# Paced first loads, and halves of the partitions exchanged by copies, in a gated mix of linear attention and a squared-ReLU MLP

## The chip, the cores and the metric

One core of a Trainium2 chip runs the whole program. The metric is device time of one execution, in microseconds (us); the times shown are the median of three runs. A profile is a further execution, with its own time. In its rows PE is TensorE's products and PEld its weight loads, DVE is VectorE, ACT ScalarE, POOL GpSimd, SP the engine that issues most transfers.

## The reference

x has 2048 rows of 448 columns. Two branches read it, and a gate for each row mixes them:

```python
qkv = (x @ wqkv).reshape(B, S, 3, 16, 28)            # q, k, v by head
phi = lambda t: where(t > 0, t + 1, exp(t)) + 1e-6
kv = einsum("bhsd,bhse->bhde", phi(k), v);  z = einsum("bhsd->bhd", phi(k))
a = (phi(q) kv / (phi(q) z + 1e-6)) @ wo             # heads joined
b = relu(x @ w1 + b1) ** 2 @ w2 + b2                 # 448 -> 1792 -> 448
g = sigmoid((x * gate_w).sum(-1))
out = g * a + (1 - g) * b
```

All in float32.

## The kernel before

**Arithmetic.** Each float32 operand is split into a rounded high part and the rest, and a product is taken as high x high, high x low and low x high. Splitting is two instructions: a cast (ScalarE or VectorE) for the high part and a subtraction (VectorE) for the low one. The 448 columns stand as four blocks of 128, the last 64 columns twice, so that the last block's high and low part use the two halves of the rows of the array.

**TensorE.** It is used as two halves of 64 rows. Each product of 128 rows is issued as two of 64, one for each half, and the halves have their own order of work (`stream[0]`, `stream[1]`). `LO` and `UP` are partitions 0 to 63 and 64 to 127.

**Stages.** Phase one takes the four blocks of 512 rows in turn: the first seven of 14 blocks of hidden units (`h_ps`, banks tagged `mm`), their down products (`o_ps`, tag `acc`), keys (`k_ps`) and the products of keys with x (`g_ps`). Then come key sums (`z_ps`), the small kv matrix, its product with wo (`kv_ps`, `m_ps`); then the blocks again for the other hidden units, queries (`q_ps`), denominators (`d_ps`) and attention (`a_ps`). Keys, queries, denominators and attention share two banks of PSUM with tag `ms`.

**What sets the order.** Nothing is ordered at run time. `Flow` is a planner: it holds a queue of operations for each engine and two lists of products, simulates them with a table of costs, and emits every instruction in the order in which the simulation starts it. `FIRST` tells it when the first 256, 512, 768 and 1024 KB have landed; `stream` starts at the time when the first product may begin; `SHIFT`, `MOVE` and `LEAVE` are tables of numbers that move single operations. Every engine then runs its list in order and waits on semaphores. The recording of all operations is one line (285) and that of all products another (420).

**The start.** TensorE begins with 15 products of 256 columns on a constant, into a bank nobody reads (line 683). SP issues eight loads of 256 KB one after the other: two that hold the first columns of w1 and x (`in_first`), then w1 and x for the other three blocks of columns, in turn. ScalarE casts the high parts; VectorE subtracts. Before the first real products the planner fills a wait with further products nobody reads (`filler`, line 684), as long as its clock is below `FILLED`.

**Halves exchanged.** At three places a sum over both halves of the partitions is needed in both: the key sums (`key_sums`), the last block of the queries (`queries_done`, `c == 3`) and the denominators' sums. There each half is transferred into the other half of another buffer by SP, and VectorE adds the two. SP's list is in order too: a transfer that waits for its data holds the loads behind it.

Of the kernel before, what the change touches and what calls it, by code (L numbers as in the profile page):

```python
# [11 lines left out]
ALU = mybir.AluOpType  # L12
# [14 lines left out]
def f32(ap):  # L27
# [8 lines left out]
FAST, FIRST = 5.2, ((262144, 3.42), (524288, 4.05), (786432, 5.1), (1048576, 6.1))  # L36
OVERLAP = {"act": 0.1, "dve": 0.085, "pool": 0.05, "sp": 0.0}

FILLED = 5.5
# [4 lines left out]
SHIFT = {"a_ps0": 7, "a_ps10": 3, "a_ps11": -10.5, "a_ps12": 11.5, "a_ps15": 10, "a_ps3": 3, "a_ps6": -1.5, "a_ps7": 26,  # L44
# [20 lines left out]
MOVE = {"a_ps0": 0.5, "a_ps1": 1.5, "a_ps10": 1.5, "a_ps12": 1.5, "a_ps13": 1.5, "a_ps14": 1, "a_ps15": -0.5, "a_ps3": 0.5,  # L65
# [11 lines left out]

LEAVE = {"a_ps0": 0, "a_ps13": -0.3, "a_ps14": 1, "a_ps15": 0.6, "a_ps2": 0.6, "a_ps3": 0.6, "a_ps5": 1, "a_ps7": 0.6,
# [13 lines left out]


class Bank:
# [89 lines left out]
class Flow:  # L184
# [138 lines left out]
    def candidate(self, name):  # L323
        best = None
        for k, op in enumerate(self.queues[name][:60]):
            if any(x.end is None for x in op.after):
                continue
# [204 lines left out]
def gated_mix_kernel(ctx: ExitStack, tc: tile.TileContext, first_in, xt, xn, wk, wq, wv, wo, w1a, w1b, w2, b1, b2, gw, hmask,  # L532
# [161 lines left out]
    for c in range(1, 4):  # L694
        load_w1(0, 0, c)
        load_x(0, c)
# [684 lines left out]
```

## Time and profile before

| what | value |
|---|---|
| median of three runs | 431.21 us (431.02 to 431.22) |
| the profiled execution | 430.65 us |
| its span, first to last instruction | 428.7 us |
| TensorE products, share of the span | 99% |
| VectorE, ScalarE | 62%, 46% |
| transfers, mean | 71 GB/s |

The span leaves out what lies before the first and after the last instruction: 1.95 us here. A row of a timeline gives start, length, engine, line, operation and shapes; in square brackets stands how long the engine was idle before and what ended it. Rows that follow each other are merged (x30), and a length then reaches from the first one's start to the last one's end. A group of instructions gives the busy time and the mean of one in ns, then the idle time before them by what ended it. A transfer's time runs from issue to landing.

### The profile page before, as it was taken

Reading aid. Unit: us, or ns where it says so; the run is one execution under the profiler, and the core shown is the slowest. Engines: PE = TensorE matmul, PEld = TensorE weight load, DVE = VectorE, ACT = ScalarE, POOL = GpSimd, SP = SyncE. Lnnn points to the kernel's source line nnn. Section 1 sums busy time; section 2 is a strip of 40 time slices with the busy share of each in tenths; the row PEclk is TensorE's granted clock in tenths of the full one; section 3 lists DMA queues with packets and bytes.
Section 4 is the critical chain, followed back from the end, with each engine's and each line's share of the span. In section 5 each row is a group of like instructions: output and inputs, shape, how many; then the busy total and the mean of one; then the engine's idle time right before and its main releaser. Section 6 shows DMA issues by size and latency. Waiting matters only on the chain.

```text
span 428.7 us, 9431 instructions
## 1 busy us (share of the span) xinstructions
PE 424.9 (99%) x3966; PEld 411.5 (96%) x3966; DVE 267.9 (62%) x517; ACT 197.2 (46%) x345; POOL 16.7 (4%) x38
## 2 busy tenths in 40 slices
PE   9999999999999999999999999999999999999997
PEld 7999999999999999999999999999999999999996
DVE  5998154934677326783764739979727695259524
ACT  6974245532365324562554456643444453364331
POOL 0000000000000000000006710000000000000000
PEclk9999999999999999999999999999999999999999
DMA  8825210141111302422325550121210310012002
GB/s 287 283 96 139 67 50 2 47 122 45 49 32 47 86 28 59 113 69 78 102 63 121 100 151 2 25 69 44 75 50 2 112 26 0 2 26 88 2 0 87
DMA packets 19802, 30.52 MB, mean 71 GB/s; under 512 B 2816, under 2 KB 14128, under 8 KB 19760
## 3 DMA queue, kind: packets, MB, share of 16 engines
q1 hardware_dynamic: 18352, 28.32, 21.5%
q0 software_dynamic: 1408, 1.61, 2.2%
q8 instruction: 31, 0.51, 0.5%
q14 instruction: 11, 0.09, 0.1%
HBM read 22.31 MB, written 3.67 MB: 61 GB/s over the span
## 4 chain that ended last, share of the span: by engine, by line
PE 99%; DVE 0%; issue 0%
PE h_ps L420 34%; PE o_ps L420 30%; PE q_ps L420 9%; PE g_ps L420 8%; PE k_ps L420 8%; PE a_ps L420 7%; PE kv_ps L420 1%; PE warm_ps L683 1%; PE m_ps L420 1%; PE e_ps L420 0%; PE d_ps L420 0%; PE z_ps L420 0%; DVE slot L285 0%; PE warm_ps L684 0%
## 5 line engine op out<-in xcount | busy, mean ns | idle before, releaser
L420 PE MATMUL h_ps<-x,w 64*128 64x512 f32 (+1 forms) x1178 | 253.8, 394 | 0.0
L420 PE MATMUL o_ps<-w_all,slot 64*128 64x448 f32 x1323 | 223.2, 361 | 0.0
L420 PEld LDWEIGHTS h_ps<-x,w 64*128 64x128 f32 x1178 | 195.0, 185 | 5.3 <-ACT w L285 0.6
L420 PEld LDWEIGHTS o_ps<-w_all,slot 64*128 64x128 f32 x1323 | 196.2, 184 | 3.3 <-PE o_ps L420 0.3
L285 DVE TENSOR_TENSOR slot<-slot,slot 128x512 fp32r<-128x512 f32 (+5 forms) x122 | 80.9, 676 | 35.4 <-ACT slot L285 24.5
L285 ACT ACTIVATE slot<-h_ps,few 128x512 f32<-128x512 f32 x56 | 38.3, 687 | 92.5 <-PE h_ps L420 82.8
L285 ACT ACTIVATE slot<-slot 128x512 f32<-128x512 f32 (+2 forms) x108 | 67.0, 628 | 9.5 <-DVE slot L285 4.7
L420 PE MATMUL q_ps<-x,wq_s 64*128 64x512 f32 x308 | 67.4, 393 | 0.0
L420 PE MATMUL k_ps<-wkm,x 64*128 64x448 f32 x336 | 66.9, 360 | 0.0
L420 PEld LDWEIGHTS k_ps<-wkm,x 64*128 64x128 f32 x336 | 57.8, 184 | 0.6
L420 PE MATMUL g_ps<-p,nh 64*128 64x448 f32 x256 | 58.3, 359 | 0.0
L420 PE MATMUL a_ps<-wkm,q 64*128 64x448 f32 x336 | 57.2, 360 | 0.0
L420 PEld LDWEIGHTS q_ps<-x,wq_s 64*128 64x128 f32 x308 | 51.4, 184 | 1.6 <-PE q_ps L420 0.3
L420 PEld LDWEIGHTS a_ps<-wkm,q 64*128 64x128 f32 x336 | 51.2, 184 | 0.6
L420 PEld LDWEIGHTS g_ps<-p,nh 64*128 64x128 f32 x256 | 42.0, 184 | 0.5
L285 DVE TENSOR_SCALAR slot<-slot 128x512 f32<-128x512 f32 (+1 forms) x35 | 14.2, 408 | 36.7 <-ACT slot L285 36.4
L420 PE MATMUL g_ps<-p,nl 64*128 64x448 f32 x96 | 31.1, 360 | 0.0
L285 ACT ACTIVATE slot<-k_ps 128x448 f32<-128x448 f32 x30 | 15.1, 541 | 31.2 <-PE k_ps L420 30.5
L285 ACT ACTIVATE slot<-q_ps 128x512 f32<-128x512 f32 x26 | 15.0, 596 | 25.7 <-PE q_ps L420 24.4
L285 POOL DMA_DIRECT2D wkm<-m x32 | 16.3, 518 | 231.0 <-ACT m L285 227.0
L285 DVE TENSOR_TENSOR gsum<-g_ps,gsum 128x448 f32<-128x448 f32 x12 | 7.5, 624 | 24.2 <-PE g_ps L420 24.2
L285 DVE CAST slot<-slot 128x512 fp32r<-128x512 f32 (+2 forms) x21 | 8.4, 401 | 21.2 <-ACT slot L285 20.9
(77 smaller groups left out, 308.2 us busy)
## 6 DMA issues: line engine op xcount, KB each, us to landing
slot<-in_xt SPq DMA_DIRECT2D x27, 256.0 KB, 2.8
slot<-in_xn SPq DMA_DIRECT2D x16, 224.0 KB, 2.6
out<-slot SPq DMA_DIRECT2D x15, 224.0 KB, 1.9
slot<-in_w SPq DMA_DIRECT2D x14, 224.0 KB, 2.8
slot<-slot SPq DMA_DIRECT2D x16, 128.0 KB, 2.4
slot<-in_w1a SPq DMA_DIRECT2D x7, 256.0 KB, 3.4
slot<-in_w1b SPq DMA_DIRECT2D x8, 192.0 KB, 3.8
wkm<-m POOLq DMA_DIRECT2D x24, 56.0 KB, 2.3
```

The lines of the kernel that those rows point to most:

```text
L285: return (lambda: method(*[real(x) for x in args], **{k: real(x) for k, x in kwargs.items()}), *self.cost(name, kind, out, ins, args))
L420: ins = pe.matmul(b.ps[where or b.whole], real(a), real(m), start=b.seen == 1 + j.whole, stop=b.seen == b.total)
L683: pe.matmul(warm_ps[:, :256], warm[:, :P], warm, start=True, stop=True)
```

## The change

Five things are done.

1. The 15 wide warm-up products become 26 of 128 columns, and `filler` goes.
2. The second to fifth load of SP wait for one of these products each (the 4th, 10th, 16th and 21st), so that SP issues them some 0.6 us apart; what stands behind on SP follows. `FIRST` and the start of `stream` get earlier times.
3. The three exchanges of halves are made by two copies of 64 partitions each, by ScalarE or VectorE as the planner chooses. For the queries the copies read PSUM, and the copy of the whole bank into SBUF goes.
4. The loads of `kvmask` and `hmask` are cut in two.
5. The planner's three tables are new, so that the order of many operations on all engines differs.

```diff
-FAST, FIRST = 5.2, ((262144, 3.42), (524288, 4.05), (786432, 5.1), (1048576, 6.1))
+FAST, FIRST = 5.2, ((262144, 2.95), (524288, 3.6), (786432, 4.3), (1048576, 5.0))
...
-FILLED = 5.5
+START = 3.45
...
-SHIFT = {"a_ps0": 7, "a_ps10": 3, "a_ps11": -10.5, "a_ps12": 11.5, "a_ps15": 10, "a_ps3": 3, "a_ps6": -1.5, "a_ps7": 26,
+SHIFT = {"a_ps0": 7, "a_ps1": 6, "a_ps11": -13.5, "a_ps12": 11.5, "a_ps15": 10, "a_ps3": 3, "a_ps4": -1.5, "a_ps6": -1.5,
...
     def candidate(self, name):
...
-            if any(x.end is None for x in op.after):
+            if any(x.end is None for x in op.after) or self.queues[name][0].behind and not op.behind:
                 continue
-            ready = max([self.now] + [x.end + SIGNAL for x in op.after])
+            ready = max([self.now] + [x.end + SIGNAL for x in op.after] + [op.behind[0] if op.behind else 0.0])
...
-        self.tc.keep_in_program_order(emit())
+        ins = self.tc.keep_in_program_order(emit())
+        if op.behind and op.behind[1]:
+            self.tc.add_manual_dep(ins.ins, op.behind[1], AFTER, reason="the loads before it keep the transfers busy")
...
     def start(self, s, j, start):
-        if start < FILLED and None is self.current[0] is self.current[1]:
-            for _ in range(int((start - max(self.stream)) / 0.107)):
-                self.tc.keep_in_program_order(self.filler())
...
-        self.stream, self.current, self.left = [3.95, 3.95], [None, None], {}
+        self.stream, self.current, self.left = [START, START], [None, None], {}
...
-    for _ in range(15):
-        pe.matmul(warm_ps[:, :256], warm[:, :P], warm, start=True, stop=True)
-    flow.filler = lambda: pe.matmul(warm_ps[:, :P], warm[:, :P], warm[:, :P], start=True, stop=True)
+    warm_up = []
+    for _ in range(26):
+        ins = pe.matmul(warm_ps[:, :P], warm[:, :P], warm[:, :P], start=True, stop=True)
+        warm_up.append(ins.ins.name)
...
+    for n, op in enumerate(flow.queues["sp"]):
+        at = 0.7 + 0.6 * min(n, 4)
+        op.behind = at, warm_up[round((at - 0.83) / 0.1067) - 1] if 0 < n < 5 else None
...
     def key_sums():
         for p in (0, 64):
-            load(r[p:p + 64], ksum[(p ^ 64):(p ^ 64) + 64])
+            copy(r[p:p + 64], ksum[(p ^ 64):(p ^ 64) + 64])
...
-            load(kvm[0], kvmask)
+            for n in (0, D // 2):
+                load(kvm[0][:, n:n + D // 2], kvmask[:, n:n + D // 2])
...
     def queries_done(b, c, ps):
         if c == 3:
-            v = slot(TB)
-            copy(v, ps)
             for p in (0, 64):
-                load(r[p:p + 64], v[p ^ 64:(p ^ 64) + 64])
-            dve.tensor_tensor(v, v, r, op=ALU.add)
+                copy(r[p:p + 64], ps[p ^ 64:(p ^ 64) + 64])
+            dve.tensor_tensor(r, ps, r, op=ALU.add)
             close(r)
-            ps, r = v, slot(TB)
-            close(v)
+            ps, r = r, slot(TB)
...
             for p in (0, 64):
-                load(r[p:p + 64], total[(p ^ 64):(p ^ 64) + 64])
+                copy(r[p:p + 64], total[(p ^ 64):(p ^ 64) + 64])
```

What the planner makes of it, at three places. In these rows `w10` is the split w1, `x0` and `x1` the high and low part of x, and a name in brackets is what the row waits for (`PE_49` TensorE, `DMAHW` a transfer, `Activation_49` ScalarE).

The first loads on SP, before and now:

```order
L285 DMA slot0_147<-in_first 128x512
L285 DMA slot1_155<-in_first 128x512
L285 DMA slot2_158<-in_w1a 128x512
L285 DMA slot3_160<-in_xt 128x512
L285 DMA slot4_162<-in_w1a 128x512
L285 DMA slot5_164<-in_xt 128x512
```

```order
L288 DMA slot0_158<-in_first 128x512
L288 DMA slot1_167<-in_first 128x512 [waits PE_49]
L288 DMA slot2_169<-in_w1a 128x512 [waits PE_49]
L288 DMA slot3_171<-in_xt 128x512 [waits PE_49]
L288 DMA slot4_175<-in_w1a 128x512 [waits PE_49]
L288 DMA slot5_180<-in_xt 128x512
```

The order of the loads is the same; four of them now wait for TensorE. The order of the casts and subtractions on ScalarE and VectorE, up to the split of `wkm`, is the same too.

The first real products on TensorE, before and now (each row is one half of the rows):

```order
L420 MATMUL h_ps0_0_173<-x0_75,w10_79 128x256 [waits DVE_49,Activation_49]
L420 MATMUL h_ps0_1_175<-x0_75,w10_79 128x256
L684 LDWEIGHTS const-bfloat16-1.0
L684 MATMUL warm_ps_85<-const-bfloat16-1.0 128x128
L684 LDWEIGHTS const-bfloat16-1.0
L684 MATMUL warm_ps_85<-const-bfloat16-1.0 128x128
L420 MATMUL h_ps0_0_173<-x0_75,w10_79 128x256 [waits Activation_49]
L420 MATMUL h_ps0_1_175<-x0_75,w10_79 128x256
L420 MATMUL h_ps0_3_189<-x0_75,w10_79 128x512 [waits Activation_49]
```

```order
L425 MATMUL h_ps0_0_178<-x0_75,w10_79 128x256 [waits DVE_49,Activation_49]
L425 MATMUL h_ps0_0_178<-x0_75,w10_79 128x256 [waits Activation_49]
L425 MATMUL h_ps0_3_193<-x0_75,w10_79 128x512 [waits Activation_49]
L425 MATMUL h_ps0_2_195<-x0_75,w10_79 128x512
L425 MATMUL h_ps0_0_178<-x1_76,w10_79 128x512 [waits DVE_49]
```

The bank `h_ps0_1`, which filled the upper half of the rows, and the fillers have left this place. Ahead of the first full-wide product, which waits for ScalarE's third cast, only the two products of `h_ps0_0` in the lower half remain. Fourteen full-wide products stand from there to the first one that reads the third and fourth load.

The fold of the first queries' last block on VectorE, now (its bank `q_ps3_3`; ahead of these rows ScalarE has made the other copy):

```order
L288 COPY slot7_3249<-q_ps3_3_3176 64x512 [waits Activation_49]
L288 TENSOR_TENSOR slot7_3249<-q_ps3_3_3176,slot7_3249 128x512 [waits DVE_49]
L288 TENSOR_TENSOR x0_75<-slot11_3222,x1_76 128x512 [waits DMAHW1_49,Activation_49]
L288 TENSOR_SCALAR slot0_3269<-slot0_3269 128x512 [waits Activation_49]
L288 TENSOR_TENSOR slot0_3269<-slot0_3269,slot1_3276 128x512 [waits DVE_49,Activation_49]
```

VectorE's copy waits for ScalarE's, and the sum for both, so the bank is read three times in a row where it was read once.

More of the change, by code (lines that the diff above doesn't have):

```diff
@@ L34 @@
 LATE, SIGNAL, TO_PE, LANDING, MOVED, SPREAD, HANDED, WAITED = 0.19, 0.04, 0.12, 1.7, 1.4, 4.0, 0.24, 0.1
-FAST, FIRST = 5.2, ((262144, 3.42), (524288, 4.05), (786432, 5.1), (1048576, 6.1))
+FAST, FIRST = 5.2, ((262144, 2.95), (524288, 3.6), (786432, 4.3), (1048576, 5.0))
 OVERLAP = {"act": 0.1, "dve": 0.085, "pool": 0.05, "sp": 0.0}
-FILLED = 5.5
+START = 3.45
 AFTER = mybir.DependencyInfo(mybir.DependencyClass.Sync, mybir.DependencyReason.DATA)
-SHIFT = {"a_ps0": 7, "a_ps10": 3, "a_ps11": -10.5, "a_ps12": 11.5, "a_ps15": 10, "a_ps3": 3, "a_ps6": -1.5, "a_ps7": 26,
[20 rows of a table removed]
-MOVE = {"a_ps0": 0.5, "a_ps1": 1.5, "a_ps10": 1.5, "a_ps12": 1.5, "a_ps13": 1.5, "a_ps14": 1, "a_ps15": -0.5, "a_ps3": 0.5,
[11 rows of a table removed]
-LEAVE = {"a_ps0": 0, "a_ps13": -0.3, "a_ps14": 1, "a_ps15": 0.6, "a_ps2": 0.6, "a_ps3": 0.6, "a_ps5": 1, "a_ps7": 0.6,
[13 rows of a table removed]
+SHIFT = {"a_ps0": 7, "a_ps1": 6, "a_ps11": -13.5, "a_ps12": 11.5, "a_ps15": 10, "a_ps3": 3, "a_ps4": -1.5, "a_ps6": -1.5,
[22 rows of a table added]
+MOVE = {"a_ps0": 0.5, "a_ps10": 1, "a_ps12": 1.5, "a_ps13": 1.5, "a_ps14": 1.5, "a_ps15": -0.5, "a_ps2": 1, "a_ps3": 0.5,
[11 rows of a table added]
+LEAVE = {"a_ps0": 0.15, "a_ps13": -0.3, "a_ps14": 1, "a_ps15": 0.6, "a_ps2": 0.6, "a_ps3": 0.6, "a_ps5": 1, "a_ps7": 0.6,
[14 rows of a table added]
 class Bank:
@@ L127, in __init__ @@
         self.takes, self.size, self.end = takes, size, None
-        self.leave, self.late = 0.0, 0.0
+        self.leave, self.late, self.behind = 0.0, 0.0, None
 class Hold:
@@ L1233, in before1 @@
                 raw = slot(P)
-                load(raw, hmask)
+                for n in (0, P // 2):
+                    load(raw[:, n:n + P // 2], hmask[:, n:n + P // 2])
                 split_hi(act, hm, raw)
```

91 rows, old and new, of tables (LEAVE, MOVE, SHIFT) are left out of this document.

## The prediction

> **What bounds the kernel now.** I read the page first: its head, the busy shares, and the chain that ended last.
>
> ```profile
> span 428.7 us, 9431 instructions
> PE 424.9 (99%) x3966; PEld 411.5 (96%) x3966; DVE 267.9 (62%) x517; ACT 197.2 (46%) x345; POOL 16.7 (4%) x38
> PE 99%; DVE 0%; issue 0%
> ```
>
> TensorE sets the end from the first microsecond to the last. So only two things can change the time: when its real products begin, and how often they wait. "Busy" does not tell the second, since a waiting product can hide behind one still draining; I count products against time instead. The chain of waits in order of time gives the steady pace; the groups of the first 10 us, shapes apart, give the count there; and the stretches up to 7.42 us (columns: length, PE, PEld and ACT busy, clock, DMA share, GB/s) split it.
>
> ```profile
> 404.55 2.33 PE h_ps L420 x20
> L420 PE MATMUL h_ps<-x,w 64*128 64x512 f32 x36 | 5.0, 409 | 0.0
> L420 PE MATMUL h_ps<-x,w 64*128 64x256 f32 x4 | 1.2, 577 | 0.0
> 4.00:5.28 1.28, 0.95 (x4) 0.66 (x6) 0.00 (x0) 1.00 1.00 306
> 5.28:7.42 2.14, 2.14 (x20) 1.93 (x19) 0.00 (x0) 1.00 1.00 348
> ```
>
> Steady: 2.33 / 20 = 0.1165 us a product (two run side by side, one in each half of the rows). By 10 us, 36 full and 4 half-wide products are worth 36 x 0.1165 + 4 x 0.058 = 4.43 us. The first began at 4.07 (next fence), so 5.93 us passed and **1.50 us** were lost. Up to 5.28 only the 4 half-wide ones ran: 0.23 us of work in 1.21, so 0.98 of the loss; the other 0.52 came later. After 10 us the list of waits has, for TensorE, little:
>
> ```profile
> PEld o_ps L420 <- PE o_ps L420: 0.3, 1, 0.3
> PEld h_ps L420 <- PE h_ps L420: 0.3, 1, 0.3
> PEld q_ps L420 <- PE q_ps L420: 0.3, 1, 0.3
> ```
>
> The h_ps one belongs to the start and the o_ps one to the last tiles, where the rows stop being split; the q_ps one, which the same view still has for 262 to 276 us alone, is the only stall of the middle. So all that this change can win is about 1.5 + 0.3 us, and part of the 1.5 is a price of the slow start, which stays. Now the start itself, in order of time:
>
> ```profile
> 0.74 0.85 SPq L285 DMA_DIRECT2D slot<-in_first  x2
> 0.78 3.36 PE L683 MATMUL warm_ps<-const-bfloat16-1.0 128*128 128x256 bf16 x15 [0.78 <-PEq L1373]
> 1.65 0.42 SPq L285 DMA_DIRECT2D slot<-in_w1a  x1
> 2.11 0.43 SPq L285 DMA_DIRECT2D slot<-in_xt  x1
> 3.50 0.42 ACT L285 ACTIVATE w<-slot 128x256 fp32r<-128x256 f32 x1 [1.48 <-DMA slot<-in_first]
> 4.07 0.58 PE L420 MATMUL h_ps<-x,w 64*128 64x256 f32 x2
> 4.10 0.42 ACT L285 ACTIVATE x<-slot 128x256 fp32r<-128x256 f32 x1 [0.19 <-DMA slot<-in_first]
> 4.43 0.40 ACT L285 ACTIVATE w<-slot 128x256 fp32r<-128x256 f32 x1
> 4.58 0.40 PE L684 MATMUL warm_ps<-const-bfloat16-1.0 128*128 128x128 bf16 x2
> 4.91 4.45 PE L420 MATMUL h_ps<-x,w 64*128 64x256 f32 x30
> 5.95 0.63 ACT L285 ACTIVATE w<-slot 128x512 fp32r<-128x512 f32 x1 [1.13 <-DMA slot<-in_w1a]
> 6.62 0.69 DVE L285 TENSOR_TENSOR w<-slot,w 128x512 fp32r<-128x512 f32 x1 [1.30 <-ACT w L285]
> ```
>
> Load, ScalarE's cast, product: the first load lets ScalarE begin at 3.50, the second at 4.10, the third only at 5.95, 4.3 us after its issue at 1.65. The warm-up products step (3.36 - 0.42) / 14 = 0.21 us for 256 columns, where a steady product takes 0.233 in its half for 512: half pace. At 5.28:7.42 the pace is full (20 rows, two of them left over from before: 18 in 2.14, 0.119 each). So half pace ends near 5.3.
>
> **The change part by part.** First, **pacing**. A load that met little else, and the third and fourth as issued now:
>
> ```profile
> DMA to landing us min/median/max: 2.6/2.8/5.3
> slot<-in_first SPq DMA_DIRECT2D x2, 256.0 KB, 2.8
> slot<-in_w1a SPq DMA_DIRECT2D x1, 256.0 KB, 4.3
> slot<-in_xt SPq DMA_DIRECT2D x1, 256.0 KB, 4.5
> 3.00:3.50 0.50, 1.00 1.07 401
> 3.50:4.00 0.50, 1.00 0.95 279
> 4.50:5.00 0.50, 1.00 0.83 283
> 8.50:9.00 0.50, 1.00 1.08 399
> ```
>
> (The first row is of all 27 loads of x, 256 KB each; the last four are stretches with clock, DMA share and GB/s.) The first load took 2.74, near the best seen: even alone it lands at 0.74 + 2.6 = 3.34 at the earliest, against 3.48. The planner's new table says 2.95; no load of this size in the trace was that quick, so I take 3.35. The second now waits for the 4th warm-up product. These are 128 wide, so they step 0.107; the two fillers of that width run 0.30 (0.40 for two, less the step). The 4th ends at 0.78 + 3 x 0.107 + 0.30 = 1.40, so the issue moves from 1.17 (0.74 + 0.43) to about 1.45. With 2.6 to 2.9 it lands at 4.05 to 4.35; now 4.08. I take 4.1: no gain. The third waits for the 10th (0.78 + 9 x 0.107 + 0.30 = 2.04, issue 2.1), the fourth for the 16th (2.69, issue 2.75), the fifth for the 21st (3.22, issue 3.27, now 2.59); the rest follow at 0.47 each on SP, so everything queued behind them is issued 0.7 later. If 2.6 to 2.9 holds for them too, the third lands at 4.7 to 5.0 (now 5.93) and the fourth at 5.35 to 5.65 (now 6.57). The bandwidth would allow it: the rate falls from 401 to 280 GB/s just when all eight are queued, and comes back later.
>
> [...]
>
> **The start.** The first product can begin at 3.37 + 0.42 + 0.15 (the lag of 3.92 to 4.07 now) = 3.9. But the order shows that ahead of ScalarE's third cast only one bank's products stand there, in one half of the rows; both halves run in full once that cast is done: second load 4.1 + 0.42 + 0.40 + 0.08 = 5.0 (now 4.91, by the same sum). Work done by 5.28: at half pace (5.28 - 5.0) / 2 = 0.14, and 0.23 / 2 for the one half's two products, 0.26 in all, against 0.23 now. So nothing up to there. After it, the waits for the third to sixth load: ScalarE's cast of the third ends near 5.5 instead of 6.58, the fourth's near 6.2 instead of 7.22, VectorE's first subtraction at 5.5 instead of 6.62. The first product on them is due after 14 others of full width: 5.28 + 14 x 0.1165 - 0.14 = 6.8. The 0.52 us should go; I keep 0.1 for VectorE, whose second subtraction ends near 6.9. **-0.42**, between +0.6 (landings late by the whole delay of issue) and -0.7 (the planner's landings, below).
>
> Would VectorE give it back later? From 10 to 20 us it is the tightest engine:
>
> ```profile
> 10.00:20.00 10.00, 10.00 (x95) 9.74 (x92) 9.79 (x20) 9.37 (x19) 0.00 (x0) 1.00 0.93 316
> ```
>
> 9.79 of 10 busy. But its chain began at 6.62 after 1.30 idle, and that start moves up by 1.0, more than the 0.42 that TensorE asks.
>
> **Copies for transfers.** Out go 16 transfers of 128 KB and 2 a little smaller, all in the second half, and four copies out of PSUM; in come 18 copies of 64 partitions, and two loads are cut in two. Prices, by the group of the nearest shape and the view of the q_ps tile:
>
> ```profile
> slot<-slot SPq DMA_DIRECT2D x16, 128.0 KB, 2.4
> L285 DVE CAST slot<-slot 128x512 fp32r<-128x512 f32 x18 | 7.7, 425 | 21.1 <-ACT slot L285 20.9
> L285 ACT ACTIVATE slot<-q_ps x26: 579/597/602, 218.9 to 375.6; 128x512 f32<-128x512 f32 x26
> L285 DVE TENSOR_SCALAR slot<-q_ps x2: 692/692/692, 230.0 to 303.4; 128x512 f32<-128x512 f32 x2
> 260.00:310.00 50.00, 50.00 (x463) 47.51 (x461) 43.76 (x74) 24.87 (x43) 0.00 (x0) 1.00 0.15 46
> ```
>
> No row has 64 partitions crossing; I take the 128-partition price (0.42 to 0.69 each, some 18 x 0.6 - 4 x 0.6 = 8.4 us over two engines and half the span), since the length of a row, not the number of rows, is what the same groups differ by; twice that would be 20 us. It hides: TensorE holds the end, and even in the fullest 50 us VectorE idles 6.2 and ScalarE 25. A query's fold shortens from 0.6 + 2.4 + 0.69 = 3.7 to 0.60 + 0.69 + 0.69 = 2.0, off the path. But its PSUM bank, free after 0.60 now, is held those 2.0 us: +1.4, four times. **0.0**, between 0 and +1.4 for each bank that TensorE needs sooner.
>
> **The new list.** It can lose the 0.3 stall or bring others; I take **-0.05**, between -0.3 and +0.6. Sum: -0.42 + 0 - 0.05 = -0.47. Span 428.7 to 428.2; with the 1.95 us around it, the profiled 430.65 becomes 430.2. The median is 431.21, 0.56 above that execution, so I forecast **430.7**.
>
> **The rivals.** 0.2% of 431.2 is 0.86 us, about what a measurement of this kernel can tell from no change.
>
> A, the planner's landings are right: 2.95 and 3.6. Then both halves run from 3.6 + 0.9 = 4.5, and by 5.28 have 0.39 + 0.12 = 0.51 against my 0.26: 0.25 more, and if the 0.3 stall also goes, about -1.0: **430.2**. For it: the drop to 280 GB/s. Against: 2.6 is the least flight seen. 0.24.
>
> B, pacing only delays: the third load flies 4.3 however late it starts, because the engines and not the queue are slow. Then all splits come 0.4 to 0.7 later: +0.5, **431.7**, within 0.2%. Against it: 2.6 to 2.8 for loads of the same size later on. 0.13.
>
> C, the slower side, the clock. The rule that fills waits before the first products with warm-up products is gone; 26 steps of 0.107 end at 3.56, and until 5.0 TensorE issues two narrow products (0.21 each) in half its rows: 1.0 us empty. If full pace has to be earned anew, from 5.0 for as long as now (0.78 to 5.3, 4.5 us), half pace lasts to 9.5: (9.5 - 5.3) / 2 = +2.1, **432.8**. It decides if that 1.0 us counts as idle. Against: now, of the 1.21 us from 4.07 to 5.28, two pairs and two fillers fill only 2 x 0.21 + 2 x 0.107 = 0.63, and 0.58 is empty. 0.07. [...]
>
> D, also slower: the bank held 1.4 us longer meets a product that needs it. One such wait is -0.47 + 1.4 = +0.9, **432.1**. For it: TensorE takes its products in a written order. Against: the planner knows the bank as taken until the last reader. 0.10.
>
> **How the numbers follow.** Forecast 0.46, with its own range 430.3 to 431.1, of which 0.04 lies beyond 0.86 us; A 0.24, B 0.13, C 0.07, D 0.10. Faster by over 0.2%: 0.28. Within: 0.42 + 0.13 = 0.55. Slower: 0.17. From 429.8 (A with 0.4 to spare) to 432.2 only C and the ends of A and D are left out.
>
> **What would show it.** Right: first cast at 3.4, second near 4.1, third near 4.9; some 4 more products begun by 10 us (0.42 / 0.1165); VectorE's first wide subtraction near 5.5. Wrong: a second cast before 3.8 (A), a third after 5.8 (B), products of 0.23 us steps after 6 us (C), TensorE waiting on VectorE or ScalarE at a q_ps bank after 214 us (D).

## The result, and the profile after

The changed kernel takes **433.47 us** (median of four, 433.07 to 433.71) against 431.12 (430.77 to 431.22) for the kernel before beside it: ratio 1.0057, 95% interval 1.0045 to 1.0070. It is slower by 2.35 us, where 430.7 was forecast. The profiled execution took 433.71 us, its span 431.9 where before's was 428.7. It is the slowest of the four, and before's profile (430.65) is quicker than before's median, so what the two traces differ by, 3.27 us, is more than 2.35.

The page's head and busy shares:

```profile
span 431.9 us, 9393 instructions
PE 427.6 (99%) x3975; PEld 413.1 (96%) x3975; DVE 274.8 (64%) x532; ACT 198.0 (46%) x344; POOL 16.7 (4%) x38
```

TensorE is as "busy" as before, and the span is 3.2 us longer: a share of 99% cannot show the loss. The start in order of time (SP's issues, TensorE's warm-up, then ScalarE's casts):

```profile
0.74 0.98 SPq L288 DMA_DIRECT2D slot<-in_first  x2
0.78 2.93 PE L686 MATMUL warm_ps<-const-bfloat16-1.0 128*128 128x128 bf16 x26 [0.78 <-PEq L1379]
2.03 0.33 SPq L288 DMA_DIRECT2D slot<-in_w1a  x1
2.67 0.33 SPq L288 DMA_DIRECT2D slot<-in_xt  x1
3.33 0.42 ACT L288 ACTIVATE w<-slot 128x256 fp32r<-128x256 f32 x1 [1.31 <-DMA slot<-in_first]
3.94 0.42 ACT L288 ACTIVATE x<-slot 128x256 fp32r<-128x256 f32 x1 [0.19 <-DMA slot<-in_first]
6.32 0.63 ACT L288 ACTIVATE w<-slot 128x512 fp32r<-128x512 f32 x1 [1.66 <-DMA slot<-in_w1a]
```

The first two casts begin 0.17 and 0.16 us earlier (3.33, 3.94), the third 0.37 later: 6.32, not near 4.9. Its load was issued at 2.03, as reckoned, and again flew 4.3 us.

The stretches of the start (columns as in the prediction), and the weight loads from 5.5 to 8 us, of after (second fence) and of before (third):

```profile
4.00:5.28 1.28, 1.24 (x4) 0.87 (x6) 1.16 (x4) 0.66 (x2) 0.00 (x0) 1.00 0.94 189
5.28:7.42 2.14, 2.14 (x10) 1.80 (x8) 0.44 (x1) 1.08 (x2) 0.00 (x0) 1.00 1.03 362
10.00:20.00 10.00, 10.00 (x90) 9.43 (x88) 8.96 (x18) 8.48 (x17) 0.00 (x0) 1.00 0.93 308
```

```profile
L425 PEld LDWEIGHTS h_ps<-x,w 64*128 64x128 f32 x12 | 2.5, 320 | 0.5
```

```profile
L420 PEld LDWEIGHTS h_ps<-x,w 64*128 64x128 f32 x20 | 2.5, 188 | 0.4
```

From 5.28 to 7.42 the row counts 10 products, where before's counted 20. A weight load takes 320 ns there instead of 188; steady it is 184. So TensorE still runs at half pace at 8 us; the trace records the grant of full pace at 8.28 us, and at 5.36 in before. (The clock column says 1.00 in both: ahead of the first grant that the trace records, it does not show the pace; the duration of a weight load does.)

Later, TensorE's waits from 20 us on:

```profile
PEld o_ps L425 <- DVE part L288: 0.5, 1, 0.5
PEld m_ps L425 <- ACT slot L288: 0.4, 1, 0.4
PEld o_ps L425 <- DVE slot L288: 0.4, 1, 0.4
PEld o_ps L425 <- issue: 0.3, 1, 0.3
PEld d_ps L425 <- DVE slot L288: 0.3, 1, 0.3
```

Before had two of 0.3 in this stretch. The old stall at a q_ps bank is gone; four new ones of 1.6 us together have come.

To see where the time went I count each real product at the steady step of its width, and add what has been lost against that to the start of the first one. This **lag** puts all runs on one scale, each by its one profiled execution:

| kernel | third load lands | full pace from | lag at 20 us | lag at 200 us | span |
|---|---|---|---|---|---|
| before | 5.93 | 5.36 | 5.74 | 5.48 | 428.7 |
| after | 6.30 | 8.28 | 7.09 | 7.44 | 431.9 |
| after_nopace | 5.63 | 8.28 | 7.15 | 7.49 | 431.6 |
| after_fill | 6.05 | 3.78 | 7.54 | 7.84 | 432.2 |
| after_true | 6.54 | 9.10 | 7.65 | 8.14 | 431.9 |
| true_oldstart | 5.77 | 6.38 | 6.86 | 7.34 | 431.6 |
| before_pace | 6.24 | 6.19 | 6.10 | 5.99 | 429.1 |
| before_gap | 6.02 | 5.31 | 6.52 | 7.09 | 430.5 |
| before_nofill | 5.90 | 6.40 | 6.02 | 5.75 | 429.0 |
| before_narrow, three executions | 6.09, 6.24, 5.40 | 3.97, 9.04, 4.26 | 5.90, 7.25, 6.01 | 5.64, 6.99, 5.54 | 429.0, 430.7, 428.6 |
| copies_retuned | 5.75 | 5.69 | 5.84 | 6.16 | 431.1 |
| copies_by_sbuf | 5.42 | 3.94 | 5.38 | 6.26 | 429.6 |
| copies_two_places | 5.61 | 3.70 | 5.48 | 5.41 | 428.7 |

After against before: +1.35 at 20 us, +1.96 at 200, +3.27 at the end of the span. So there are three things to explain: the first 20 us; 0.6 more up to 200 us, where of the halves only those of the key sums are exchanged (at 192.7); and 1.3 behind that. The 0.6 is not all loss. The changed kernel makes its eight products of the key sums, each only two columns wide, at 196.4 to 199.8 us, before makes them at 211.4 to 213.2, and a count by width takes them for almost nothing. Counted at 195 us, ahead of them in both, some 0.4 have been added since 20 us, and 1.5 are left for what follows.

### The profile page after: what moved, and what is told of

It is laid out like the page before. It is cut to its first block, busy times and chain, and to the rows that moved or that the text cites. A ratio compares the mean times of both kernels' runs of the same rounds, so it can differ in the third digit from the quotient of the medians.

```text
span 431.9 us, 9393 instructions
## 1 busy us (share of the span) xinstructions
PE 427.6 (99%) x3975; PEld 413.1 (96%) x3975; DVE 274.8 (64%) x532; ACT 198.0 (46%) x344; POOL 16.7 (4%) x38
## 4 chain that ended last, share of the span: by engine, by line
PE 96%; DVE 2%; ACT 1%; DMA 1%; issue 0%; ACTq 0%
PE h_ps L425 34%; PE o_ps L425 29%; PE q_ps L425 8%; PE k_ps L425 8%; PE g_ps L425 8%; PE a_ps L425 7%; DVE slot L288 1%; PE m_ps L425 1%; DMA slot<-in_first 1%; ACT slot L288 1%; PE kv_ps L425 0%; PE e_ps L425 0%; DVE part L288 0%; PE d_ps L425 0%; DVE x L288 0%
## 5 line engine op out<-in xcount | busy, mean ns | idle before, releaser
L425 PE MATMUL o_ps<-w_all,slot 64*128 64x448 f32 x1323 | 227.7, 362 | 0.2 <-DVE part L288 0.2
L425 PEld LDWEIGHTS o_ps<-w_all,slot 64*128 64x128 f32 x1323 | 198.8, 184 | 4.4 <-DVE part L288 0.5
L288 DVE TENSOR_TENSOR slot<-slot,slot 128x512 fp32r<-128x512 f32 (+5 forms) x118 | 77.9, 675 | 33.0 <-ACT slot L288 30.4
L288 ACT ACTIVATE slot<-slot 128x512 f32<-128x512 f32 (+3 forms) x108 | 67.2, 628 | 17.1 <-DVE slot L288 10.2
L425 PE MATMUL a_ps<-wkm,q 64*128 64x448 f32 x336 | 65.0, 361 | 0.0
L425 PEld LDWEIGHTS k_ps<-wkm,x 64*128 64x128 f32 x336 | 59.2, 184 | 0.7
L425 PEld LDWEIGHTS a_ps<-wkm,q 64*128 64x128 f32 x336 | 56.6, 184 | 1.1
L288 ACT ACTIVATE slot<-a_ps,gate 128x448 f32<-128x448 f32 x16 | 10.1, 633 | 36.3 <-PE a_ps L425 32.5
L288 ACT ACTIVATE slot<-q_ps 128x512 f32<-128x512 f32 (+1 forms) x28 | 15.9, 593 | 21.8 <-PE q_ps L425 18.8
L288 DVE SCALAR_TENSOR_TENSOR part<-part,gate,slot 128x448 f32<-128x448 f32 x12 | 8.2, 684 | 26.1 <-ACT slot L288 26.1
```

Of the source, the lines that this page charges most:

```text
L288: return (lambda: method(*[real(x) for x in args], **{k: real(x) for k, x in kwargs.items()}), *self.cost(name, kind, out, ins, args))
L425: ins = pe.matmul(b.ps[where or b.whole], real(a), real(m), start=b.seen == 1 + j.whole, stop=b.seen == b.total)
```

## The experiments

### The pacing

after_nopace takes only the waits of the loads out of the changed kernel; before_pace puts only them into the kernel before (loads two to five wait for the 2nd, 5th, 8th and 11th of its wide products).

```diff
-        op.behind = at, warm_up[round((at - 0.83) / 0.1067) - 1] if 0 < n < 5 else None
+        op.behind = at, None
```

```diff
+    for n, op in enumerate(flow.queues["sp"]):
+        if 0 < n < 5:
+            op.behind = warm_up[(1, 4, 7, 10)[n - 1]]
```

> The changed kernel with the same lists on all engines, but no load waits for a warm-up product, so SP issues the eight loads back to back. Theory (hole in TensorE's work): full pace still near 8.3; the third load lands at 5.9 in place of 6.3, which at half pace gains little: 433.0 to 433.5. Rival 2 (the loads are the loss): 431.9 to 432.3. If pacing helps as its planner says: over 433.8.

> The kernel before with its wide warm-up products and fillers, and the second to fifth load made to wait for the 2nd, 5th, 8th and 11th wide product (ends near 1.4, 2.05, 2.7 and 3.3 us, as in the change). Theory: full pace near 5.4; the third load flies some 4.3 us again and lands near 6.3, so TensorE waits 0.3 to 0.5 longer: 431.4 to 431.7. Rival 2 (the loads are the whole loss): 432.5 or more. If pacing helps: third load by 5.0, 430.6 to 430.8.

after_nopace: 433.54 us (432.81 to 434.00), ratio to before 1.0053 [1.0036, 1.0071]. before_pace: 431.32 (430.98 to 432.09), 1.0002 [0.9991, 1.0014]. In after_nopace, ScalarE's third cast comes 0.67 earlier than in after:

```profile
5.65 0.63 ACT L288 ACTIVATE w<-slot 128x512 fp32r<-128x512 f32 x1 [0.89 <-DMA slot<-in_w1a]
```

So pacing delays the third load by about as much as it delays its issue (the paced kernels have it at 6.05 to 6.54, most of the unpaced ones at 5.4 to 5.9), and it neither gains nor costs anything that can be measured. before_gap holds the third load alone, for the 12th wide product:

```diff
+        if n == 2:
+            op.behind = warm_up[11]
```

> The kernel before; only the third load waits, for the 12th wide warm-up product, so that SP issues it near 3.6 us, when the first has landed, and what stands behind follows. If a load's flight is long because it was issued into full queues (the prediction's step), it takes 2.6 to 3 us again and lands at 6.2 to 6.6, hardly later than now (5.93). If a third load flies 4.3 us however late it starts (rival B), it lands at 7.9, TensorE waits 1.5 to 2 us more for it, and the time is 432 to 433.

432.06 us (431.85 to 432.62), 1.0025 [1.0016, 1.0034]. Its issue and ScalarE's third cast:

```profile
3.53 0.33 SPq L285 DMA_DIRECT2D slot<-in_w1a  x1
...
6.04 0.63 ACT L285 ACTIVATE w<-slot 128x512 fp32r<-128x512 f32 x1 [1.25 <-DMA slot<-in_w1a]
```

Issued at 3.53, it lands at 6.02: a flight of 2.5 us, and a landing within 0.1 us of the one that before issued at 1.65. So both readings in the prediction were half right: a load issued as the queues run empty (99 GB/s from 3.50 to 3.75, then 0 to 4.25) does fly 2.5, but nothing issued between 1.65 and 3.53 landed earlier for waiting. What the gap costs, 0.9 us, fits the loads behind: the fifth lands at 8.55 instead of 7.24, and TensorE waits 1.0 us in two pieces for VectorE's subtractions that follow, where before has no such wait.

### The warm-up

after_fill adds two narrow warm-up products, and fills the holes behind them with four more. before_narrow is the kernel before with the 26 narrow products and no fillers; before_nofill keeps its 15 wide ones and loses only the fillers.

```diff
+        self.made = getattr(self, "made", 0) + 1
+        for _ in range({2: 3, 3: 1}.get(self.made, 0)):
+            tc.keep_in_program_order(self.filler())
...
-    for _ in range(26):
+    for _ in range(28):
```

```diff
-        if start < FILLED and None is self.current[0] is self.current[1]:
+        if False and None is self.current[0] is self.current[1]:
...
-    for _ in range(15):
-        pe.matmul(warm_ps[:, :256], warm[:, :P], warm, start=True, stop=True)
+    for _ in range(26):
+        pe.matmul(warm_ps[:, :P], warm[:, :P], warm[:, :P], start=True, stop=True)
```

> The changed kernel with TensorE's holes at the start filled by products nobody reads: 28 narrow warm-up products in place of 26, 3 more behind the first real product and 1 behind the second. Theory (the hole between the warm-up and the first full-wide products makes full pace come at 8.3 us and not near 5.4): full pace returns to 5.2 to 5.6, and of the 1.45 us (half of 2.9) some 0.5 goes to waits for the third load, so 432.4 to 432.8. Rival 1 (narrow warm-up products do not count as the wide ones do): full pace stays near 8.3, 433.3 to 433.6. Rival 2 (the late third load is the whole loss): no change, 433.3 to 433.6, with full pace at 5.4 all the same.

> The kernel before with 26 narrow warm-up products in place of 15 wide ones, no filler behind the first products, and nothing else changed. Theory (hole) and rival 1 (narrow products): full pace near 8.3, and the time longer by 1.0 to 1.5 us, 432.1 to 432.6. If neither holds and full pace is a matter of chance: 431.0 to 431.3 with full pace near 5.4.

> The kernel before with its 15 wide warm-up products but without the two fillers behind the first products. If holes behind the warm-up decide when full pace comes: a share of executions near 433, as with the narrow warm-up without fillers (432.6 median, 431.0 to 433.6). If it is the narrow products, or the end of the warm-up at 3.6 in place of 4.0: 430.9 to 431.3, like the kernel before.

before_nofill: 430.91 us (430.16 to 432.13), 0.9999 [0.9988, 1.0009]: the fillers do nothing. before_narrow: 432.56 median, 1.0027 [1.0009, 1.0045], and its ten executions lie apart: three at 431.0 to 431.2, two at 431.9 and 432.1, five at 433.0 to 433.6. The profile fell on a quick one (431.08, full pace from 3.97), so the same kernel was profiled again under two other names.

> The kernel before with 26 narrow warm-up products and no fillers, once more, for its profile. Rival C: an execution of 432.8 or more shows full pace only at 7.5 to 10 us, one near 431 shows it by 6.5. If the time and the point of full pace do not go together, the spread has another cause.

> The same kernel a third time. Rival C: 432.8 or more goes with full pace at 7.5 to 10 us, near 431 with full pace by 6.5; otherwise another cause.

They took 432.75 and 430.65 us, with full pace from 9.04 and from 4.26. Their weight loads from 5.5 to 8 us, the slow one first:

```profile
L420 PEld LDWEIGHTS h_ps<-x,w 64*128 64x128 f32 x14 | 2.5, 322 | 0.5
```

```profile
L420 PEld LDWEIGHTS h_ps<-x,w 64*128 64x128 f32 x23 | 2.3, 184 | 0.4
```

One program, two paces, 2.1 us apart; 1.24 of it stands in the lag at 20 us already and 1.45 at 200, the rest is in later waits that fell differently. That is rival C: with the narrow warm-up full pace is sometimes not granted near 4 us, and then only after 8. Of the seven profiles with 26 narrow products five show it at 8.28 to 9.90, two near 4; all nine with the wide ones (fillers or not) have it by 6.40. That leaves open what in the warm-up decides: its products are narrower, it is shorter (2.93 us for 3.36), and it ends earlier (3.71 for 4.14); no run parts these. Nor is before quite free of it, perhaps: one of its 75 executions beside these runs took 433.1, without a profile, where all others lie at 430.1 to 431.6.

But early full pace does not mend the changed kernel. after_fill has it at 3.78 and takes 434.23 us (433.67 to 434.52), 1.0067 [1.0040, 1.0093], where my theory expected 432.4 to 432.8. Its waits from 4.8 to 12 us:

```profile
PEld h_ps L428 <- ACT x L288: 1.3, 1, 1.3
PEld h_ps L428 <- DVE x L288: 0.5, 1, 0.5
```

Fourteen full-wide products at full pace are soon done (2.23 us, from 5.08), and then TensorE stands 1.3 us before the fourth load, which landed at 7.44 in this execution. A second limit lay just behind the first.

### The list at the start

The changed kernel's first products ask for the third and fourth load after 16 products, before's after 23, since its planner is told 4.3 and 5.0 us for landings that come at 6.3 and 6.95. after_true tells it the measured ones; true_oldstart gives that list the start of before as well (15 wide products, two fillers, no pacing).

```diff
-FAST, FIRST = 5.2, ((262144, 2.95), (524288, 3.6), (786432, 4.3), (1048576, 5.0))
+FAST, FIRST = 5.2, ((262144, 3.38), (524288, 4.0), (786432, 6.25), (1048576, 6.9))
...
-START = 3.45
+START = 3.85
...
-"h_ps0_1": 1.5
+"h_ps0_1": -2
```

> The changed kernel, its planner told the landings that its own trace shows (3.38, 4.0, 6.25, 6.9 us, start 3.85) and the bank h_ps0_1 put back to its old place among the first products; all else as in the change, so the planner makes another list of the same tables. The first product that needs the third and fourth load then stands behind 22 products of the first block and not behind 16 (23 in the kernel before). Theory (the list asks for those loads too early, because it was made for landings at 4.3 and 5.0): the loss counted by 20 us falls by about 1 us against the change, to that of the paced kernel before (start of the first product plus loss: 6.1, against 7.1 in the change); with full pace at 8.3 about 6.5. Rival (the loads alone): no less than 7.0. The later part of the list is another one and may keep its 1.5 to 1.9 us: 432.0 to 432.9 in all.

> The changed kernel's list, made for landings as measured (3.4, 4.0, 6.25, 6.9), with the start of the kernel before: 15 wide warm-up products, two fillers, loads not paced. With the changed start the same list took 433.9, with full pace only at 9.1 us. Theory (the start's part is the warm-up): full pace by 6.5 us, TensorE at 20 us where before is (within 0.4 us, against 1.9 us late), and 432.2 to 432.8 in all, the rest being the list behind 20 us. Rival (the start's loss is in the order of the first products and splits): it stays 1.3 us or more behind at 20 us, 433.5 or above.

after_true: 433.91 us (433.73 to 434.13), 1.0070 [1.0052, 1.0088], with full pace only at 9.10; 432.0 to 432.9 was expected. true_oldstart: 433.54 (432.93 to 433.70), 1.0054 [1.0039, 1.0069]. My theory expected at most 432.8; the rival was right. It has before's warm-up, full pace at 6.38, and its third load lands earlier than before's (5.77), yet its lag at 20 us is 6.86 against 5.74. Some 0.3 of that may be the pace, since before_nofill, with full pace at 6.40, stands at 6.02; the other 0.8 come with the list, whatever the warm-up and the loads. That the list asks for the third and fourth load too early cannot be what costs them: in after_true and true_oldstart 22 products stand ahead, against 23 in before. Nor are they all in the first products. About half of the 0.8 arises between 18 and 20 us: a product of one half of the rows starts at 18.59 and its next one only at 19.48, for it waits for a bank of keys (k_ps) that the other half still fills, a product every 0.2 us. No view of waits shows this, because TensorE as a whole is busy. The rest of the 0.8 was not traced; the planner's own account ends this list near 427.8 us, and before's at 425.6. The table says it more broadly: at 200 us, ahead of the queries, all five kernels of the table with a list of the change's making stand at 7.3 to 8.1, whatever their start; those with the list of before and full pace by 6.4 stand at 5.5 to 6.0, before_gap apart. In the changed kernel the clock hides behind the list, and the list behind the clock: no run that undid one gained anything.

### The copies

First the plain swaps: before_copies puts only the copies into the kernel before, after_dma puts only the transfers back into the changed one. Both keep the tables of numbers of the kernel that they came from.

```diff
-                load(r[p:p + 64], total[(p ^ 64):(p ^ 64) + 64])
+                copy(r[p:p + 64], total[(p ^ 64):(p ^ 64) + 64])
```

> The kernel before with the three exchanges of halves made by copies, as in the change, and nothing else: start, warm-up, tables and loads as before. Theory (copies hide, the old tables take them well enough): 430.7 to 431.6. Rival (the copies are what costs after 20 us, since a 64-partition copy takes VectorE as long as one of 128): TensorE waits for VectorE at d_ps, o_ps or m_ps, 432.0 or more.

> The changed kernel with its new tables and paced start, but the three exchanges by transfers as before. The start is the same (loss by 20 us as in the change). If the copies cost what is lost after 20 us, that part falls from 1.9 to under 0.8 us over the kernel before, 432.2 to 432.6. If it is the tables, it stays at 1.5 or more, 433.1 to 433.9 (the tables belong to the other operations, so it can also get worse).

before_copies: 434.92 us (434.67 to 435.49), 1.0095 [1.0080, 1.0111]. after_dma: 434.85 (434.35 to 435.65), 1.0094 [1.0076, 1.0111]. Both ways lose, so neither says anything clean of copies: the tables fit the operations they were made for. So I made tables anew for three kernels that keep before's start untouched, with its first 60 products in the same order: copies_retuned copies at all three places; copies_two_places copies the key sums and the denominators' sums and transfers the queries' block as before; copies_by_sbuf has the tables of copies_retuned, and its very list up to 220 us, but first copies the query bank whole into SBUF, so that the two copies read that.

```diff
         if c == 3:
+            v = slot(TB)
+            copy(v, ps)
             for p in (0, 64):
-                copy(r[p:p + 64], ps[p ^ 64:(p ^ 64) + 64])
-            dve.tensor_tensor(r, ps, r, op=ALU.add)
+                copy(r[p:p + 64], v[p ^ 64:(p ^ 64) + 64])
+            dve.tensor_tensor(v, v, r, op=ALU.add)
```

> The kernel before, its start untouched (15 wide warm-up products, fillers, unpaced loads, the same first 60 products), with the copies at all three places in place of transfers and with numbers of the three tables that fit them: by the planner's own account its last product starts at 425.7 us, as in the kernel before (425.6), against 430.1 for the same copies with the numbers of before, which took 434.9. If the 1.9 us that the changed kernel loses after 20 us are the list and not the copies, this runs within 0.2% of before, 430.6 to 431.9, with half pace over by 6.5 us. If copies cost in themselves (a port, VectorE and ScalarE that come late), some 1.5 to 2 us of waits of TensorE return after 210 us: 432.5 to 433.2.

> As the run beside it, but the last block of the queries keeps its transfers, so only the key sums and the denominators' sums are copied; numbers for this, last product planned at 425.2, 0.4 before that of the kernel before. Theory (what the list plans is what it gives, to some 0.3 us): 430.5 to 431.2, same or a little faster. Rival (copies cost in themselves): slower than before by 0.5 to 1 us.

> As copies_retuned (all three exchanges by copies, the same tables, the same list up to the first exchange of queries at 220 us), except that the last query block is first copied whole into SBUF, as in the kernel before, and the two copies of 64 partitions read that: one more operation of 0.6 us a block, but the bank is free after 0.6 us and not after 2.0. The planner ends both at the same time, 425.7. Rival D (the held bank): the waits of TensorE of 0.41 us at 222.4 and 0.60 us at 303.5 go and the time falls from 433.1 to 432.1 or below. If it is only how well the list fits: 432.8 to 433.5, with waits of the same size at these or other places.

| kernel | us (range) | ratio to before |
|---|---|---|
| copies_retuned | 433.14 (432.79 to 435.00) | 1.0054 [1.0041, 1.0068] |
| copies_by_sbuf | 431.88 (431.33 to 432.20) | 1.0023 [1.0014, 1.0032] |
| copies_two_places | 430.88 (430.27 to 431.67) | 0.9994 [0.9986, 1.0003] |

Reading the bank once instead of three times is worth some 1.0 us, each kernel against the executions of before beside it (+2.00 for copies_retuned, +1.03 for copies_by_sbuf). The first fold of copies_retuned, in order of time:

```profile
220.26 0.59 ACT L306 ACTIVATE slot<-q_ps 64x512 f32<-64x512 f32 x1 [4.58 <-PE q_ps L441]
...
220.89 0.69 DVE L306 COPY slot<-q_ps 64x512 f32<-64x512 f32 x1 [1.65 <-ACT slot L306]
221.61 0.69 DVE L306 TENSOR_TENSOR slot<-q_ps,slot 128x512 f32<-128x512 f32 x1
...
222.42 0.18 PEld L441 LDWEIGHTS q_ps<-x,wq_s 64*128 64x128 f32 x1 [0.41 <-issue]
```

Three reads follow each other from 220.26 to 222.30; the next product into a bank of this tag starts its weights at 222.42, after 0.41 us of nothing. Its row names no releaser, but the time fits the end of the sum, and ScalarE goes on at 222.42 too. The second such wait, at 303.51, is 0.60. In copies_by_sbuf the same bank is free after one read,

```profile
220.42 0.60 ACT L306 ACTIVATE slot<-q_ps 128x512 f32<-128x512 f32 x1 [4.54 <-PE q_ps L441]
```

and both waits are gone. TensorE's waits behind 20 us that only one of the two kernels has, in copies_retuned (first fence) and in copies_by_sbuf (second):

```profile
PEld a_ps L441 <- issue: 0.6, 1, 0.6
PEld q_ps L441 <- issue: 0.4, 1, 0.4
```

```profile
PEld o_ps L441 <- ACT slot L306: 0.6, 1, 0.6
PEld o_ps L441 <- DVE slot L306: 0.3, 1, 0.3
```

The 0.41 and 0.60 make up the 1.0. The two of copies_by_sbuf lie ahead of 60 us, before any half is exchanged. The rest of what both kernels lose is mostly their list's: ahead of all copies, at 200 us, they stand at 6.16 and 6.26 against before's 5.48. In the changed kernel itself the view of the q_ps tile has one such wait, before the denominators' product that takes the next bank, and the prices of the copies:

```profile
L288 ACT ACTIVATE slot<-q_ps x28: 577/594/599, 220.5 to 378.2; 128x512 f32<-128x512 f32 x23, 64x512 f32<-64x512 f32 x5
L288 DVE TENSOR_TENSOR slot<-q_ps,slot x4: 684/692/692, 221.9 to 354.4; 128x512 f32<-128x512 f32 x4
L288 DVE COPY slot<-q_ps x3: 685/685/694, 221.2 to 303.5; 64x512 f32<-64x512 f32 x3
...
PEld d_ps L425: 0.3, 1
```

No run tied the other new waits of the changed kernel (m_ps, o_ps) to a single operation: before_copies has waits of that kind (2.0 us at o_ps for VectorE and ScalarE), after_dma, with transfers, has none of them, but each has another list. With the query block left to transfers and tables made for it, copies cost nothing and gain nothing (ratio 0.9994). The loads of the masks, cut in two, were not tried alone. No kernel here is measurably faster than the kernel before; copies_two_places equals it.

## Why the prediction was wrong

**What bounds it** held: TensorE from end to end, and the loss in its start and a few waits.

**Pacing, 0.52 us to go.** This step failed first: "If 2.6 to 2.9 holds for them too, the third lands at 4.7 to 5.0". The issue times came as reckoned (1.39, 2.03, 2.67, 3.21 for 1.45, 2.1, 2.75, 3.27), the first landing too (3.31 for 3.35), the second gained 0.16 where nothing was expected; but the third flew 4.27 us and landed at 6.30, the fourth at 6.95. The 2.6 us came from loads that found the queues idle, later in the program (the one issued at 122.31 us, with a DMA share of 0.05 in the 1.3 us before it). before_gap shows that a load issued 2.35 us behind the one ahead does fly 2.5 us; 0.64 us is not such a gap. At the spacing of the change this was rival B, with 0.13 (its "however late" fell with before_gap), and by its own price it would have left the time at 431.7. after_nopace and before_pace show that pacing costs nothing measurable either: the step that failed took away the gain, and the loss came from the terms below, put at nothing or nearly so.

**The start.** "So nothing up to there" held at 5.28, and then the gain of 0.42 became a loss of 1.35. Two things were missed. The term for the clock took half pace to end at 5.3 in any case; it ended at 8.28. Rival C had the effect and its price (+2.1; the two executions of before_narrow are 2.1 apart; the changed kernel's own lag at 20 us is 1.35 more), with a chance of 0.07. My argument against it, that before has holes of the same kind between 4.07 and 5.28, missed the point: before_nofill confirms that those holes and their fillers do not matter (ratio 0.9999). What differs is the warm-up, 2.93 us of it at narrow products and 3.36 at wide ones. That one program has full pace at 3.97, 4.26 and 9.04 us shows that the moment varies from execution to execution. What in the warm-up makes the late case common is not shown. That 2.93 us are too short for an early one is not shown either, and copies_two_places speaks against it: it has full pace at 3.70, 2.9 us after its first product.

The second miss is the order of the products. "Fourteen full-wide products stand from there to the first one that reads the third and fourth load" was counted, and then used only with a landing at 4.7 to 5.0. With the landing where it was, the shorter run of products is a loss as soon as the pace is full, which the wait of 1.3 us in after_fill shows. It is not the whole of the list's part: true_oldstart, with 22 products ahead, still has its 0.8, of which one half of the rows standing idle near 19 us is about half and the rest stays open.

**Copies, 0.0.** The prices were right: 594 and 685 ns for 64 partitions are those of 128, and the work hides on two engines, as copies_two_places shows. The bank was right in its time (+1.4, 2.0 us held) and wrong in its effect: "the planner knows the bank as taken until the last reader" does not mean that it finds other work for TensorE. This is rival D, at 0.10 and +0.9 for a wait; copies_retuned against copies_by_sbuf measures 1.0 for two. In the changed kernel its list meets only one, of 0.3, so this mechanism is a small part of the loss there.

**The new list, -0.05.** This term had the wrong sign: some 0.8 of the first 20 us, if true_oldstart may stand for the changed kernel; 0.4 from there to 195 us, where the change does little but order anew; and, as far as no run ties them to the copies, the waits after that (1.6 us, for one old stall of 0.3). Of the range given to it, -0.3 was the old stall, and +0.6 came from no row. The planner's own account could have told: its last product is planned at 425.6 us in the kernel before and at 426.2 in the changed one, although that believes in a start 0.5 us earlier.

**The chances.** C, D and a worse list came together, and they were priced as if one at a time; the range, to 432.2, ends below every one of them joined to another.

## What to carry to other kernels

Before a load is held back for the sake of another's flight, see where a load with that much distance landed in the same traffic; a flight measured on idle queues does not carry over (2.6 us there, 4.27 here). A warm-up that is made shorter or narrower has to be judged by when full pace comes, and since that varies from run to run (3.97, 4.26 and 9.04 us here) it takes several profiles of one kernel: the weight loads' duration (320 or 184 ns here) tells the pace at once. When a shared bank is released by a chain of small reads instead of one, count the chain's length (2.0 us here, against 0.6 for the one read, and two waits of 0.41 and 0.60) as time for which TensorE needs other work. Where the array works as two halves, count products against time, since a half that waits leaves no mark in the busy share (10.00 us busy of the 10 from 10 to 20 us in before and after alike, with 95 products and 90). And when tables that order the work come with an operation, try that operation only with tables of its own.

## What the runs showed that was not expected

The third load of 256 KB landed at 5.93, 6.30 and 6.02 us when it was issued at 1.65, 2.03 and 3.53 (before, after, before_gap; over all runs at 5.40 to 6.24 when issued at 1.65). What holds it until then was not found.

Within a list, a late or early start is partly evened out: copies_retuned and copies_by_sbuf have the same list up to 220 us, and starts 0.46 us apart at 20 us (5.84, 5.38) stand at 6.16 and 6.26 at 200. Full pace at 3.97 and 4.26 instead of 5.36 was worth nothing at 200 us in before's list (5.64 and 5.54 against 5.48), while full pace at 9.04 cost 1.5 (6.99).
